# Windowed attention and a mixture of adapters: load tiles cut by key block and head instead of by running rows

## The chip, the cores and the metric

The kernel runs on one NeuronCore of one Trainium2 chip. Its engines are TensorE (PE; PEld is its weight load), VectorE (DVE), ScalarE (ACT), GpSimd (POOL) and SyncE (SP, which here only issues DMAs). The core has 16 DMA engines. The metric is the device time of one execution in microseconds; the time before is the median of three runs. A profile is of one more execution.

## The reference

q, k and v are float32 arrays of shape (8 batches, 8 heads, 576 rows, 64). The reference computes, in short:

```python
scores = q @ k.T / sqrt(64)                 # for each batch and head, 576 x 576
scores = where(abs(i - j) <= 32, scores, -1e9)
x = softmax(scores) @ v                     # (8, 8, 576, 64)
x = x.transpose(0, 2, 1, 3).reshape(4608, 512)
logits = x @ w_gate                         # 8 experts
topk, w = two best experts, softmax over their logits
out = x + sum over the two of w * ((x @ A[e]) @ B[e])   # A[e]: 512 x 16, B[e]: 16 x 512
```

Only a band of 65 keys counts for each query, so a block of 64 keys meets 128 queries at most, and a block of 128 queries meets three key blocks. The inputs are 28.3 MB, the output 9.4 MB.

## The kernel before

**Pairs.** Batch b and batch b + 4 are worked on together: one in partitions 0 to 63, the other in 64 to 127. So there are 32 units (4 pairs of batches x 8 heads) of 576 rows.

**Loads** (`load_qk` line 281, `load_v` line 321). The rows of all units are taken as one run of 18432 rows and cut into nine tiles of 2048 rows, without regard to where a head ends. A q or k tile is one DMA of 1 MB (line 288, on SP): each of 128 partitions takes 16 consecutive rows of each of the two batches, 4 KB each. Each half of it (8 rows per partition) is cast to f16 (line 299 on POOL or DVE, 297 on ACT), transposed by eight PE matmuls (line 307) into a PSUM bank, and copied into `qT` or `kT` (line 317). A v tile comes in four DMAs of 32 partitions (line 329, on POOL, which casts to f16 on the way) and is turned by one DVE transpose (line 338). The weights of the adapters come on SP once k tile 2 has been asked for (lines 253 to 258).

**Scores** (`score`, line 376). 36 tiles of eight key blocks. Two matmuls write the mask into two PSUM banks (line 393), then K^T Q is added for each block and each batch of the pair (line 398); a block whose queries lie in two q tiles takes two matmuls. ACT takes the exponential into `PT` (line 405). For the first three pairs of batches the blocks go head by head, for the last pair four heads go head by head and four block by block.

**PV** (`pv`, line 414). Up to five items (a unit and a block of 128 queries) share two PSUM banks (line 435); column 64 of v is 1 and gives the softmax sum. DVE takes the reciprocal (line 447) and writes the normalized x (line 460).

**Adapters** (`moe`, line 476). x is transposed (line 488), multiplied with all A and w_gate at once (line 529), the gate goes through nine small DVE and ACT operations (lines 539 to 560), the gated product (line 570) is transposed (579) and multiplied with all B (line 607). x is added on DVE (line 621, first pair) or by an identity matmul (line 610) with a copy on ACT or DVE (line 618). The store is on SP (line 628). Such a chain is made for ten blocks of 128 rows at once in the first three pairs of batches, and for 4, 4 and 2 blocks in the last: six chains.

**Order.** Nothing is scheduled at run time. `ORDER` lists all operations, `ON` says on which engine each runs where there is a choice, and `HOME` gives each buffer its place in its pool. Each engine works through its own operations in that order, and an instruction that waits holds up all behind it on its engine; for SP and POOL that includes the DMAs that they issue. A load also waits for a free `raw` buffer (five of 1 MB) or `v16` buffer (three). The order was written by a planner that isn't part of the kernel; durations given to `op` are its estimates and do nothing at run time.

Of the kernel before, what the change touches and what calls it, by code (L numbers as in the profile page):

```python
# [19 lines left out]
NUN = 32  # L20
NSLOT = NUN * NB
NTILE = NSLOT // 32
SB = 4
GS = 188
# [22 lines left out]
class Op:  # L47
    def __init__(self, eng, fn, bufs, need, make, prio, dma):
        self.eng, self.fn = eng, fn
        self.bufs, self.need, self.make = bufs, need, make  # L50
        self.prio, self.dma = prio, dma
        self.mode, self.count = 0, 0
        self.on, self.given = None, False


class Plan:
# [14 lines left out]
    def op(self, eng, dur, fn, bufs=(), need=(), make=(), prio=0.0, dma=0.0, mode=0, count=0):  # L71
        eng = eng if isinstance(eng, dict) else {eng: dur}
        o = Op(eng, fn, list(bufs), list(need), list(make), prio, dma)
        o.mode, o.count = mode, count
# [30 lines left out]
def kernel(  # L105
# [14 lines left out]
    POOLS = {"B": 8, "raw": 5, "c16": 6, "v16": 3,  # L120
             "qT": 3, "kT": 3, "vt": 3, "PT": 7, "xs": 2, "xT": 1, "zs": 2, "zT": 2, "ob": 4,
# [4 lines left out]
    def many(name, shape, dt, pool=sb):  # L126
# [6 lines left out]
        "qT": many("qT", [128, 2048], F16),  # L133
# [3 lines left out]
        "xs": many("xs", [128, 2, 5, DD], F16),  # L137
        "xT": many("xT", [128, 10, 4, 128], F16),
        "zs": many("zs", [128, 5, ER], F16),
        "zT": many("zT", [128, 5, 128], F16),  # L140
        "ob": many("ob", [128, 2, DD], F32),
        "sm": many("sm", [128, 280], F32),
        "rc": many("rc", [128, 5, 2, 1], F32),
# [54 lines left out]
    op("POOL", 3.5, build_mask, make=["mask"], prio=-98)  # L198
# [10 lines left out]
    op("POOL", 1.6, build_twice, make=["mask"], prio=-97)  # L209
# [35 lines left out]
    for i, t in enumerate(phys["vt"]):  # L245
# [7 lines left out]
    op("SP", 0.4, lambda: nc.sync.dma_start(  # L253
        out=waf, in_=moe_A.rearrange("e (p c) r -> p e (c r)", c=4)),
        bufs=[wb], need=[("k", 2, "raw")], make=["waf"], prio=LATE_W, dma=0.262)
    op("SP", 0.4, lambda: nc.sync.dma_start(
        out=wgf, in_=moe_w_gate.rearrange("(p c) e -> p c e", c=4)), need=[("k", 2, "raw")], make=["waf"], prio=LATE_W, dma=0.02)
    op("SP", 0.4, lambda: nc.sync.dma_start(
        out=bf, in_=moe_B.rearrange("e r d -> (e r) d")), bufs=[wb], need=[("k", 2, "raw")], make=["bf"], prio=LATE_W, dma=0.262)

# [8 lines left out]
    qrows = {"q": q, "k": k, "v": v}  # L269

    def run_view(w):

        return qrows[w].rearrange("(g b) h (n r) d -> (b h n) g (r d)", g=2, r=16)

    def v_view():

        return qrows["v"].rearrange("(g b) h (s f r) d -> (b h s) f g (r d)", g=2, f=2, r=32)

    qT, kT, vt = {}, {}, {}

    def load_qk(w, t):
        raw = buf("raw", f"raw{w}{t}")
        src = run_view(w)[128 * t:128 * t + 128]
        due = 32 * t if t else -100
        late = 0 if w == "q" else 1
        dst = buf(w + "T", f"{w}T{t}")
        (qT if w == "q" else kT)[t] = dst
        op("SP", 0.46, lambda: nc.sync.dma_start(out=ap(raw), in_=src),
           bufs=[raw], make=[(w, t, "raw")], prio=-80 + due + late if t else -200 + late, dma=DMA_MB)
        for hf in range(2):  # L290
            c16 = buf("c16", f"{w}16_{t}_{hf}")

            def cast(eng, hf=hf, c16=c16):
                o = ap(c16).rearrange("p r (g d) -> p r g d", g=2)
                i = ap(raw).rearrange("p g (f r d) -> p f r g d", f=2, d=D)[:, hf]
# [6 lines left out]
               need=[(w, t, "raw")], make=[(w, t, hf, "16")], prio=due - 30 + late + 0.1 * hf)  # L302
            tp = buf("B", f"tp{w}{t}_{hf}")

            def trans(hf=hf, c16=c16, tp=tp):
                for r in range(8):
                    nc.tensor.matmul(out=ap16(tp)[:, 128 * r:128 * r + 128], lhsT=ap(c16)[:, r],  # L307
                                     rhs=ident, is_transpose=True, start=True, stop=True)
# [4 lines left out]
            def evict(eng, hf=hf, tp=tp):  # L313

                o = ap(dst).bitcast(F32).rearrange("m (x f r) -> m f x r", f=2, r=8)[:, hf]
                i = ap(tp).rearrange("m (r x) -> m x r", r=8)
# [3 lines left out]

    def load_v(t):
        v16, dst = buf("v16", f"v16_{t}"), buf("vt", f"vt{t}")
        vt[t] = dst
        src = v_view()
        due = 32 * t if t else -90
        for g in range(2):
            for f in range(2):
                p0 = 64 * g + 32 * f
                op("POOL", 0.62, lambda p0=p0, f=f, g=g: nc.gpsimd.dma_start(  # L329
                    out=ap(v16)[p0:p0 + 32], in_=src[32 * t:32 * t + 32, f, g]),  # L330
                    bufs=[v16],
# [9 lines left out]
    for t in range(NTILE):  # L341
        load_qk("q", t)
        load_qk("k", t)
        load_v(t)


    seq = []
    for s in range(SB):
        us = list(range(8 * s, 8 * s + 8))
        if s < SB - 1:  # L350
            seq += [(u, a) for u in us for a in range(NB)]
        else:
            seq += [(u, a) for u in us[0:4] for a in range(NB)]
            seq += [(u, a) for a in range(NB) for u in us[4:8]]
    place = {ua: divmod(i, 8) for i, ua in enumerate(seq)}
    PT = {}

    def slot(u, a):
        return divmod(NB * u + a, 32)

    def run_deps(kind, u, row0, row1):

        r = set()
        for row in range(row0, row1, 32):
            t, c = divmod(NB * 64 * u + row, 2048)
            r.add((kind, t))
        return r

    def score(ti):
        ps = buf("B", f"ps{ti}", 2)  # L370
        PT[ti] = pt = buf("PT", f"PT{ti}")
        blocks = seq[8 * ti:8 * ti + 8]
        need, bufs, n = {"mask", "ident"}, {ps}, 0
        parts = []
# [369 lines left out]
```

## Time and profile before

| | before |
|---|---|
| median of 3 runs | 140.14 us (139.21 to 140.89) |
| the profiled execution | 138.75 us |
| its span | 137.0 us |
| mean granted TensorE clock | 0.969 |
| PE busy | 110.1 us (80%) |
| DVE, ACT, POOL busy | 90.3, 85.3, 49.9 us |
| moved by DMA | 33.90 MB; HBM read 28.85 MB, written 9.44 MB |
| q and k loads | 18 of 1024 KB, median 12.6 us (k) and 15.7 us (q) from issue to landing |
| v loads | 36 of 128 KB, 7.1 us to landing |

The page of the profile divides the span into 40 slices: a digit is the busy share in tenths. A line of the DMA part gives a queue with its packets, megabytes and the time that its packets took, as a share of 16 engines over the span; q1 is the queue of SP, q0 that of POOL. The megabytes of v count what is written (f16); twice as much is read. Matmuls are pipelined, so PE's busy time also holds the ends of overlapping matmuls; in the chain that ended last a matmul stands with the time from its start to the next one's.

### The profile page before, as it was taken

What the parts mean: (1) busy time and instruction counts of PE and PEld (TensorE: products, weight loads), DVE (VectorE), ACT (ScalarE), POOL (GpSimd) and SP (SyncE); (2) the same over time, 40 slices, a digit from 0 to 9 for tenths busy, and PEclk for the clock granted to TensorE, in tenths of its full rate; (3) what the DMA queues carried; (4) which work ended last, traced back from release to release, by engine and by line L of the source; (5) the groups of instructions that cost most, each with busy time, mean ns of one, the idle gap of its engine ahead of it and who ended that gap; (6) DMA issues with size and microseconds to landing.
All of it is one profiled execution on the core that took longest, in us unless ns stands there. A gap on an engine that the chain in (4) does not pass through costs nothing.

```text
span 137.0 us, 5167 instructions
## 1 busy us (share of the span) xinstructions
PE 110.1 (80%) x2238; PEld 82.2 (60%) x2238; DVE 90.3 (66%) x182; ACT 85.3 (62%) x124; POOL 49.9 (36%) x84
## 2 busy tenths in 40 slices
PE   5934777949599979299929999769999999999800
PEld 2324456637498857277717796746868676875300
DVE  2323757368586895758838987929596979768700
ACT  7104399726669697248726767748946885678620
POOL 7992187059553960559401995000000000000000
PEclk9997799999999999779999999999999999999997
DMA  4999999999999999979999499700960300636993
GB/s 100 378 292 291 360 408 334 335 384 388 255 300 386 403 299 290 286 273 251 284 326 425 89 215 232 206 13 11 334 235 5 115 5 7 234 115 240 311 369 115
DMA packets 13222, 33.90 MB, mean 247 GB/s; under 512 B 2704, under 2 KB 2704, under 8 KB 13200
## 3 DMA queue, kind: packets, MB, share of 16 engines
q1 hardware_dynamic: 11472, 28.86, 57.5%
q0 software_dynamic: 1728, 4.72, 19.4%
q8 instruction: 17, 0.28, 0.8%
q14 instruction: 5, 0.04, 0.1%
HBM read 28.85 MB, written 9.44 MB: 280 GB/s over the span
## 4 chain that ended last, share of the span: by engine, by line
PE 44%; DMA 35%; issue 6%; DVE 5%; ACT 3%; POOL 2%; SPq 1%; POOLq 0%; ACTq 0%; DVEq 0%
DMA raw<-in_k_dram 19%; DMA raw<-in_q_dram 14%; PE banks L435 9%; PE banks L398 8%; PE banks L307 6%; PE banks L488 5%; PE banks L529 5%; PE banks L607 4%; PE banks L393 4%; PE banks L610 3%; DMA out_dram<-ob 3%; POOL c L299 2%; ACT ob L618 1%; DVE xs L460 1%; PE banks L579 1%
## 5 line engine op out<-in xcount | busy, mean ns | idle before, releaser
L405 ACT ACTIVATE PT<-banks 128x1024 f16<-128x1024 f32 x36 | 36.2, 1024 | 12.4 <-PE banks L398 11.6
L299 POOL CAST c<-raw 128x1024 f16<-128x1024 f32 x27 | 27.5, 1046 | 33.1 <-DMA raw<-in_k_dram 14.6
L307 PE MATMUL banks<-ident,c 128*128 128x128 f16 x288 | 22.1, 230 | 11.1 <-POOL c L299 5.6
L307 PEld LDWEIGHTS <-c 128*128 128x128 f16 x288 | 18.3, 103 | 14.9 <-POOL c L299 6.8
L460 DVE TENSOR_TENSOR xs<-banks,rc 128x640 f16<-128x640 f32 (+1 forms) x33 | 26.4, 802 | 1.1
L398 PE MATMUL banks<-qT,kT 64*64 64x128 f16 (+3 forms) x608 | 22.8, 216 | 1.7 <-issue 1.4
L398 PEld LDWEIGHTS <-kT 64*64 64x64 f16 x608 | 17.4, 108 | 10.3 <-issue 9.9
L338 DVE STREAM_TRANSPOSE vt<-v 128x1024 f32<-128x1024 f32 x9 | 18.7, 2079 | 5.3 <-DMA v<-in_v_dram 5.3
L435 PE MATMUL banks<-vt,PT 64*128 64x65 f16 x832 | 17.5, 190 | 4.6 <-issue 3.7
L435 PEld LDWEIGHTS <-PT 64*128 64x128 f16 x832 | 14.5, 94 | 7.2 <-issue 5.3
L329 POOL DMA_DIRECT2D v<-in_v_dram x36 | 17.7, 499 | 0.1
L618 ACT COPY ob<-banks 128x1024 f32<-128x1024 f32 (+1 forms) x14 | 12.5, 928 | 5.3 <-PE banks L610 3.7
L607 PE MATMUL banks<-Bw,zT 128*128 128x512 f16 x40 | 14.9, 393 | 0.4 <-ACT zT L180 0.4
L393 PE MATMUL banks<-mask,twice 64*128 64x512 f16 x72 | 14.1, 386 | 0.6 <-ACT PT L405 0.4
L447 DVE RECIPROCAL rc<-banks 128x10 f32<-128x10 f32 (+1 forms) x33 | 7.1, 214 | 11.3 <-PE banks L435 10.1
L297 ACT CAST c<-raw 128x1024 f16<-128x1024 f32 x6 | 6.3, 1050 | 9.9 <-DMA raw<-in_q_dram 9.9
L317 ACT COPY kT<-banks 128x512 f32<-128x512 f32 x15 | 8.8, 592 | 5.2 <-PE banks L307 5.1
L610 PE MATMUL banks<-xs,ident 128*128 128x512 f16 x30 | 11.4, 379 | 0.0
L529 PE MATMUL banks<-WA,xT 128*128 128x136 f16 x160 | 10.8, 223 | 0.3 <-issue 0.3
L488 PE MATMUL banks<-ident,xs 128*128 128x128 f16 x160 | 10.8, 219 | 0.1
L488 PEld LDWEIGHTS <-xs 128*128 128x128 f16 x160 | 9.8, 114 | 1.4 <-DVE xs L460 0.2
L529 PEld LDWEIGHTS <-xT 128*128 128x128 f16 x160 | 9.8, 98 | 1.3 <-issue 0.5
(49 smaller groups left out, 97.5 us busy)
## 6 DMA issues: line engine op xcount, KB each, us to landing
raw<-in_k_dram SPq DMA_DIRECT2D x9, 1024.0 KB, 12.6
raw<-in_q_dram SPq DMA_DIRECT2D x9, 1024.0 KB, 15.7
out_dram<-ob SPq DMA_DIRECT2D x24, 256.0 KB, 3.4
v<-in_v_dram POOLq DMA_DIRECT2D x36, 128.0 KB, 7.1
out_dram<-ob SPq DMA_DIRECT2D x16, 192.0 KB, 3.0
ob<-in_moe_A_dram SPq DMA_DIRECT2D x1, 256.0 KB, 17.5
ob<-in_moe_B_dram SPq DMA_DIRECT2D x1, 256.0 KB, 10.7
wgf<-in_moe_w_gate_dram SPq DMA_DIRECT2D x1, 16.0 KB, 16.6
```

The costliest lines, as they stand in the source:

```text
L299: (nc.vector if eng == "DVE" else nc.gpsimd).tensor_copy(out=o, in_=i)
L307: nc.tensor.matmul(out=ap16(tp)[:, 128 * r:128 * r + 128], lhsT=ap(c16)[:, r], rhs=ident, is_transpose=True, start=True, stop=True)
L329: op("POOL", 0.62, lambda p0=p0, f=f, g=g: nc.gpsimd.dma_start(out=ap(v16)[p0:p0 + 32], in_=src[32 * t:32 * t + 32, f, g]), bufs=[v16], ma ...
L338: nc.vector.transpose(out=o, in_=i)
L393: nc.tensor.matmul(out=p[:, 4 * j:4 * j + 4], lhsT=twice[m], rhs=bcast(mask[m], 1, 4), start=True, stop=False)
L398: nc.tensor.matmul(out=p[m, i, c0:c0 + w], lhsT=ap(kT[t])[m, 64 * s:64 * s + 64], rhs=ap(qT[tq])[m, c:c + w], start=False, stop=(n == len( ...
L405: op("ACT", act(1024), lambda: nc.scalar.activation(out=ap(pt)[:, :, 64:192].rearrange("m i (x b r) -> m i x b r", b=2, r=16), in_=ap(ps). ...
L435: nc.tensor.matmul(out=ap(po)[:, 512 * g + VD * j:512 * g + VD * j + VD], lhsT=ap(PT[ti])[m, pos, off:off + 128], rhs=ap(vt[t])[m, sl, 0:V ...
L460: nc.vector.tensor_tensor(out=o, in0=i, in1=ap(rc)[:, 0:n].to_broadcast([128, n, 2, D]), op=ALU.mult)
L488: nc.tensor.matmul(out=ap16(tp)[:, 512 * i + 128 * c:512 * i + 128 * c + 128], lhsT=ap(xs[s])[:, b, g].rearrange("p (m c) -> p c m", c=4)[ ...
L529: nc.tensor.matmul(out=ap(pz)[:, o:o + ER + E], lhsT=ap(xT)[:, i, c, :], rhs=WA[:, c, :], start=(c == 0), stop=(c == 3))
L607: nc.tensor.matmul(out=o, lhsT=ap(zT)[:, j + i], rhs=Bw, start=True, stop=not by_pe)
```

## The change

- **q and k loads.** The tiles are cut by batch pair, row range and head. Tile t < 8 holds pair t // 2, all eight heads, and 256 rows of each: four key blocks for k; for q the range is shifted by 32 rows. Tile 8 holds what is left over of all 32 units: the ninth key block of k, and the first and last 32 rows of q. Runs are of 8 rows, 2 KB. Each half of a tile and each batch of the pair has a DMA of its own (256 KB; for q tile 8 each end too, 128 KB): 76 loads on SP instead of 18. `raw` has nine buffers of 512 KB instead of five of 1 MB.
- **v loads** are cut the same way, still four DMAs a tile on POOL.
- **Queries.** `qT` is one buffer for a pair of batches, [head, 576 rows], two in all. q tile 8 goes to a buffer `xq`, from which one copy per pair (`ends`) fills in the first and last 16 columns of pairs (32 rows) of each head.
- **Scores.** A tile is one key block of all eight heads; no block is split any more.
- **PV** takes items block by block, seven groups of 5 or 6 a pair instead of eight (nine in the last). x lies in two buffers, blocks 0 and 1 in `xa`, blocks 2 to 4 in `xb`.
- **Adapters.** Two chains for each pair, of 4 and 6 blocks of 128 rows: eight chains. The softmax pieces lie elsewhere in PSUM and SBUF.
- **Weights** are loaded from ACT's queue at the start.
- **Order.** `ORDER`, `ON` and `HOME` are new, 594 operations instead of 553. The last q or k load on SP is the first half of k tile 6, behind 12 of the 40 stores.

```diff
-    POOLS = {"B": 8, "raw": 5, "c16": 6, "v16": 3,
-             "qT": 3, "kT": 3, "vt": 3, "PT": 7, "xs": 2, "xT": 1, "zs": 2, "zT": 2, "ob": 4,
+    POOLS = {"B": 8, "raw": 9, "c16": 6, "v16": 3, "xq": 1,
+             "qT": 2, "kT": 4, "vt": 4, "PT": 7, "xa": 2, "xb": 1, "xT": 1, "zs": 2, "zT": 2, "ob": 4,
...
-        "raw": many("raw", [128, 2, 16 * D], F32),
+        "raw": many("raw", [128, 2, 8 * D], F32),
...
-    op("SP", 0.4, lambda: nc.sync.dma_start(
+    op("ACT", 0.5, lambda: nc.scalar.dma_start(
         out=waf, in_=moe_A.rearrange("e (p c) r -> p e (c r)", c=4)),
...
+    grows = {w: x.rearrange("(g b) h n d -> g b h n d", g=2) for w, x in (("q", q), ("k", k), ("v", v))}
...
+    def run_parts(w, t, f):
+
+        r = []
+        for g in range(2):
+            x = grows[w][g]
+            if t < XT:
+                r0 = 256 * (t % 2) + (32 if w == "q" else 0)
+                i = x[t // 2, :, r0:r0 + 256].rearrange("h (n f r) d -> f h n (r d)", f=2, r=8)[f]
+                r.append((g, 0, 128, i))
+            elif w == "k":
+                i = x.rearrange("b h n d -> (b h) n d")[:, 512:576].rearrange(
+                    "u (n f r) d -> f u n (r d)", f=2, r=8)[f]
+                r.append((g, 0, 128, i))
+            else:
+                for e in range(2):
+                    i = x.rearrange("b h n d -> (b h) n d")[:, 544 * e:544 * e + 32].rearrange(
+                        "u (n f r) d -> f u n (r d)", f=2, r=8)[f]
+                    r.append((g, 64 * e, 64, i))
+        return r
...
-        op("SP", 0.46, lambda: nc.sync.dma_start(out=ap(raw), in_=src),
-           bufs=[raw], make=[(w, t, "raw")], prio=-80 + due + late if t else -200 + late, dma=DMA_MB)
         for hf in range(2):
+            raw = buf("raw", f"raw{w}{t}_{hf}")
+            for n, (g, p0, np_, src) in enumerate(run_parts(w, t, hf)):
+                op("SP", 0.46, lambda g=g, p0=p0, np_=np_, src=src, raw=raw: nc.sync.dma_start(
+                    out=ap(raw)[p0:p0 + np_, g], in_=src),
+                   bufs=[raw], make=[(w, t, "raw", hf)],
...
+                if w == "q" and t < XT:
+                    c0 = 16 + 128 * (t % 2)
+                    o = ap(dst).bitcast(F32)[:, :, c0:c0 + 128].rearrange(
+                        "m h (x f r) -> m f h x r", f=2, r=8)[:, hf]
+                    i = ap(tp).rearrange("m (r h x) -> m h x r", r=8, h=NH)
...
+    def ends(s):
+
+        def go(eng):
+            w = ap(qT[s]).bitcast(F32)
+            o = dataclasses.replace(w, ap=[list(w.ap[0]), [272, 2], [288, NH], [1, 16]])
+            i = ap(xq).bitcast(F32).rearrange("m (e u r) -> m e u r", e=2, r=16)[:, :, NH * s:NH * s + NH]
+            (nc.scalar.copy if eng == "ACT" else nc.gpsimd.tensor_copy)(out=o, in_=i)
...
-                op("POOL", 0.62, lambda p0=p0, f=f, g=g: nc.gpsimd.dma_start(
-                    out=ap(v16)[p0:p0 + 32], in_=src[32 * t:32 * t + 32, f, g]),
+                x = grows["v"][g]
+                if t < XT:
+                    r0 = 256 * (t % 2)
+                    src = x[t // 2, :, r0:r0 + 256].rearrange("h (a f r) d -> f h a (r d)", f=2, r=32)[f]
+                else:
+                    src = x.rearrange("b h n d -> (b h) n d")[:, 512:576].rearrange(
+                        "u (f r) d -> f u (r d)", f=2)[f]
+                op("POOL", 0.5, lambda p0=p0, src=src: nc.gpsimd.dma_start(
+                    out=ap(v16)[p0:p0 + 32], in_=src), bufs=[v16],
...
+            for h in range(NH):
+                sl = slot(NH * s + h, a)[1]
                 for g in range(2):
                     m = slice(64 * g, 64 * g + 64)
...
+                    nc.tensor.matmul(out=p[m, h, c0:c0 + hi - lo], lhsT=ap(kT[t])[m, 64 * sl:64 * sl + 64],
+                                     rhs=ap(qT[s])[m, h, lo:hi], start=False, stop=h % 4 == 3)
...
     for s in range(SB):
+        for i0, n in ((0, 6), (6, 5), (11, 5), (16, 6), (22, 6), (28, 6), (34, 6)):
+            pv(s, i0, n)
...
     for s in range(SB):
-        e = 72 * (s + 1)
-        if s < SB - 1:
-            moe(s, [(b, g) for b in range(2) for g in range(5)], e + 16, 10)
-        else:
-            moe(s, [(b, g) for g in (0, 1) for b in range(2)], 72 * s + 66, 4)
-            moe(s, [(b, g) for g in (2, 3) for b in range(2)], 72 * s + 82, 4)
-            moe(s, [(b, g) for g in (4,) for b in range(2)], 72 * s + 90, 4)
+        moe(s, [(b, g) for g in (0, 1) for b in range(2)], 72 * s + 46, 4)
+        moe(s, [(b, g) for g in (2, 3, 4) for b in range(2)], 72 * s + 86, 4)
```

More of the change, by code (lines that the diff above doesn't have):

```diff
@@ L319, in load_qk @@
                bufs=[tp, dst], need=[(w, t, hf, "T")], make=[(w + "T", t)], prio=pr)
+    def ends(s):
[4 more added lines that the diff above has]
+            (nc.scalar.copy if eng == "ACT" else nc.gpsimd.tensor_copy)(out=o, in_=i)
+        op({"POOL": 0.45, "ACT": act(256)}, 0, go, bufs=[xq, qT[s]], need=[("qT", XT)], make=[("ends", s)],
+           prio=due_of(2 * s) + (24 if s == 0 else -10))
     def load_v(t):
@@ L428, in pv @@
                 need |= {("PT", ti), ("vt", t)}
-        last = max(x[1] for x in ops)
+        last = 9 * s + max(x[1][1] for x in ops)
         def go():
```

246 lines of the change are left out of this document (107 added, 139 removed), and 86 rows, old and new, of tables (HOME, ORDER).

## The prediction

> **What bounds the kernel now.** I read the page first, then the stretches of the span, then the chain that ended last in order of time, and last the DMA view of the first 20 us. From the page:
>
> ```profile
> span 137.0 us, 5167 instructions
> PE 110.1 (80%) x2238; PEld 82.2 (60%) x2238; DVE 90.3 (66%) x182; ACT 85.3 (62%) x124; POOL 49.9 (36%) x84
> PE   5934777949599979299929999769999999999800
> DMA  4999999999999999979999499700960300636993
> DMA packets 13222, 33.90 MB, mean 247 GB/s; under 512 B 2704, under 2 KB 2704, under 8 KB 13200
> q1 hardware_dynamic: 11472, 28.86, 57.5%
> q0 software_dynamic: 1728, 4.72, 19.4%
> PE 44%; DMA 35%; issue 6%; DVE 5%; ACT 3%; POOL 2%; SPq 1%; POOLq 0%; ACTq 0%; DVEq 0%
> DMA raw<-in_k_dram 19%; DMA raw<-in_q_dram 14%; PE banks L435 9%; PE banks L398 8%; PE banks L307 6%; PE banks L488 5%; PE banks L529 5%; PE banks L607 4%; PE banks L393 4%; PE banks L610 3%; DMA out_dram<-ob 3%; POOL c L299 2%; ACT ob L618 1%; DVE xs L460 1%; PE banks L579 1%
> ```
>
> The DMA row stands at 9 for the first half, PE's row at 7 to 9 for the second, and the chain divides likewise: a third of the span waits for q and k loads, then it is TensorE. The stretches say it with numbers (columns: stretch, length, busy us of PE, PEld, DVE, ACT, POOL, granted clock, DMA share, GB/s):
>
> ```profile
> 10.00:20.00 10.00, 6.38 (x104) 4.82 (x106) 5.45 (x7) 5.47 (x8) 3.80 (x8) 0.83 1.04 348
> 20.00:30.00 10.00, 7.49 (x188) 5.56 (x180) 6.70 (x9) 6.46 (x9) 5.00 (x7) 1.00 1.03 347
> 30.00:40.00 10.00, 8.23 (x247) 6.70 (x248) 6.47 (x13) 7.17 (x9) 7.19 (x10) 1.00 1.07 330
> 40.00:50.00 10.00, 9.35 (x171) 8.22 (x169) 8.06 (x19) 8.00 (x15) 6.63 (x11) 1.00 1.03 358
> 85.00:95.00 10.00, 8.14 (x221) 6.12 (x220) 7.31 (x15) 6.76 (x10) 0.00 (x0) 1.00 0.33 86
> 115.00:125.00 10.00, 9.92 (x138) 7.08 (x136) 7.88 (x28) 7.02 (x12) 0.00 (x0) 1.00 0.50 179
> ```
>
> Until 50 us all 16 DMA engines are full (a share of 1.03 to 1.07: the packets of an engine overlap by about 5%). After the loads the share falls to 0.3 to 0.5, and PE is full.
>
> **How a copy is dealt to the engines.** The packet counts can be taken apart. The q and k loads are 18 x 256 runs of 4 KB, the stores 4608 rows of 2 KB, the weights 1024 + 128 + 128 packets. That leaves 11472 - 10496 = 976 = 61 x 16 on q1, which has 61 issues. On q0 the 36 v loads have 32 rows each: 1728 - 1152 = 36 x 16. So every copy of this kernel closes with 16 small packets, one for each engine. The outermost counts of these copies are 128, 96 and 32, all multiples of 16, so each engine gets an equal number of rows.
>
> **The change, part by part.**
>
> *Loads.* A run is now 8 rows (2 KB), and for t < 8 the source of a q or k load is x[t // 2, :, r0:r0+256], written as h, n, (r d). The 256 rows of a head end before the next head begins, so heads and runs don't merge: the outermost count is **8 heads**, where it was 128 runs. There are 8 tiles x 2 tensors x 2 halves x 2 groups = 64 such copies of 256 KB. The v loads of t < 8 are "h a (r d)", 8 outermost too. Only tile 8 (left-over rows, 32 pairs of batch and head outermost) keeps a multiple of 16.
>
> No row shows a copy with 8 outermost. If it is dealt as the 97 copies of the trace are, in equal shares of the outermost count, there are eight shares of one head each, and eight of the 16 engines carry the load. That is my likeliest case: three different counts obey it. The bounds are 16 engines (as now) and eight.
>
> By a rule of the Trainium skill (page "DMA: Bandwidth & Descriptors", section "Why a DMA increments its semaphore by 16 and not by 1") a copy runs on the largest number up to 16 that divides the slowest dimension of both sides; on the hardware queue these are the lowest-numbered engines, on the software queue consecutive ones from a cursor that goes round. By that rule the 64 loads fall on the same eight engines each time, and the v loads alternate between the halves, which is the case that I sum below. The trace agrees for 128, 96 and 32; no run here shows 8 yet. With 16 engines instead the sum would be that of the first rival.
>
> The price. q1's packets took 0.575 x 16 x 137.0 = 1260 engine-us for 28.86 MB: 43.7 per MB, so 11.45 for a copy of 256 KB. The lower bound for 2 KB runs is the best slice of q and k loads:
>
> ```profile
> DMA  0009269999999999999999999999999999999999
> GB/s 0 0 0 106 25 197 434 434 401 393 418 303 303 303 262 361 270 311 295 311 279 271 279 270 328 295 270 279 402 287 295 418 410 401 418 410 393 434 410 418
> ```
>
> 434 GB/s over 16 engines is 36.9 us per MB. q1's mean holds as many 2 KB packets (stores) as 4 KB ones, so I take it, divided by the overlap of 1.05. What the eight busiest engines must carry before the last q or k load has landed:
> - 64 loads: 64 x 11.45 / 8 = 91.6 us (over 16 engines it would be 45.8)
> - tile 8 of q and k, 2.10 MB over 16: 5.7; weights, 0.54 MB: 1.5
> - v: 0.194 x 16 x 137.0 = 425 engine-us, on an average engine 26.6
> - stores: in the new order 12 of 40 (2.88 MB) stand ahead of the last load (k tile 6, first half) on SP: 7.9
>
> Sum 133.3, over 1.05 = 127.0. The first load gives the start:
>
> ```profile
> 0.74 4.98 DMA raw<-in_k_dram
> ```
>
> 1 MB over 16 engines takes 2.9 of these 4.98 us, so data flows from 0.74 + 2.1 = 2.8 us. The last load lands at about **130 us**; in the kernel before DMA was no longer full by 85 us.
>
> Do queues leave these engines idle? SP issues 116 copies instead of 61 at some 0.4 us, 50 us in 130. A load waits on SP for a raw buffer, and there are nine of 512 KB, up to 18 copies or 26 us of work ahead. The stores on SP wait for adapter chains and hold back the loads behind them; but those chains need tiles that were issued more than ten copies earlier, so the reserve covers them. I take no idle time; without that cover it is a few us.
>
> *What is left after the last load.* k tile 6 holds the first four key blocks of the last batch pair. Its second group of transposes stands on PE ahead of all nine score tiles of that pair. Before, the like point is the last k transposes:
>
> ```profile
> 105.05 0.45 PE banks L307 x8
> 108.45 0.51 PE banks L435 x26
> 108.96 0.21 PE banks L393 x2
> 109.17 0.56 PE banks L398 x16
> 121.62 0.22 PE banks L607
> 121.83 0.22 PE banks L610
> 122.05 0.95 PE banks L529 x16
> 123.00 0.22 PE banks L579 x4
> 123.22 0.45 PE banks L488 x8
> 124.57 1.02 ACT ob L618
> 127.25 3.44 DMA out_dram<-ob
> 130.79 1.01 ACT ob L618
> ```
>
> From 105.5 to the end are 31.5 us. By these rows PE still had 6 score tiles (0.78: 4.7 us), 208 PV matmuls (4.1), 40 transposes (2.25), 40 low-rank matmuls (2.4), 20 of zs (1.1) and 10 pairs of output matmuls at 0.87 (8.7): 23.2 us. The other 8.3 are waits: for a softmax, for norm on DVE, the last gate chain, and the output copy with its store. After the change there stand behind that point 9 score tiles (7.1), 264 PV matmuls (5.2), 64 transposes (3.6), 64 low-rank matmuls (3.8), 16 of zs (0.9), 8 transposes of q (0.45) and the output matmuls of both chains of the last two pairs, 40 (8.7): 29.7 us. With the same 8.3 of waits 38.0. Before it come the cast and the transposes:
>
> ```profile
> L299 POOL CAST c<-raw 128x1024 f16<-128x1024 f32 x27 | 27.5, 1046 | 33.1 <-DMA raw<-in_k_dram 14.6 <-DMA raw<-in_q_dram 13.1 <-PE banks L307 4.7
> L237 ACT COPY PT<-zt__115 128x256 f32<-128x256 f32 x8 | 2.7, 398 | 0.0
> L557 DVE RECIPROCAL sm<-sm 128x10 f32<-128x10 f32 x3 | 0.6, 216 | 0.1
> L553 DVE SCALAR_TENSOR_TENSOR sm<-sm,banks 128x80 f32<-128x80 f32 x3 | 0.7, 230 | 0.4 <-ACT banks L547 0.4
> ```
>
> 1.05 + 0.45 + 0.1 between them = 1.6.
>
> *The other parts* are small and lie under the load waits. Score tiles of whole blocks: 608 matmuls become 576, 1.1 us less PE at 0.56 / 16. Reciprocal and norm run 28 times instead of 33, on the same elements: about 1 us less DVE. Eight chains instead of six: 80 small DVE operations instead of 69, 11 x 0.22 = 2.4 us more DVE. The four copies of left-over queries are like the copy of 256 elements in the row above: 4 x 0.4, on POOL and ACT. The weights now come first, on ACT's queue: their 1.5 us are in the sum. The q eviction writes another pattern with the same 512 elements; neither gain nor loss is excluded, 18 x 0.1 us either way is my bound. If PE bound throughout they would be worth about 2 us; with PE waiting for data, nothing.
>
> **Sum.** 129.8 + 1.6 + 38.0 = 169.4 us of span. The profiled execution took 138.75 for its span of 137.0, 1.75 around it, and lies 1% under the median of 140.14. So 171.2; **forecast 171 us**, 1.22 times the median before. With 36.9 us per MB in place of 43.7 / 1.05 the loads end at 115 and it is 157; without overlap they end at 136 and it is 178, and some 5 us of idle queues make 183.
>
> **Rivals.**
> 1. *All 16 engines carry the new loads*, whether a copy is cut below the head or eight shares wander over the engines. For it: the DMA rows show nothing but even use. Against it: every copy that they show has an outermost count that 16 divides. Then the engine time is (733 + 91 + 24 + 425 + 126) / 16 / 1.05 = 83.3 us, the last load lands at 86, and 86.1 + 1.6 + 38.0 + 1.75 = **127 us**, up to 135 if PE, with some 66 us of work before that point, isn't ready by then. This is the side on which it is faster; it decides whenever the 64 loads use more than about 12 engines, where their term falls from 91.6 to 61 and the time to about 142.
> 2. *The v loads fall on one half.* They are eight heads outermost as well. If they all sit on the engines of the q and k loads, 32 / 36 of 26.6 = 23.6 us come twice: + 22.5, **194 us**. If they all sit on the other eight, 22.5 less: 149. Nothing in the rows speaks for either.
> 3. *The change isn't what ends last*: that the reordered tail with its last chain of six items costs more than the 8.3 us of waits. It is 3 us at most (a third gate chain of about 2 us is gone, an add per pair remains), inside the range of every case.
>
> **How the numbers follow.** Forecast's case, 157 to 183: 0.70. Rival 1: 0.13. Rival 2: 0.12, half on each side. The remaining 0.05 is for stalls on SP or POOL beyond the reserve, above 183. The range 150 to 195 holds the forecast's case and most of rival 2, a little over 8 in 10, and leaves rival 1 out. Faster by over 1% (about what a measurement of this kernel tells from no change) has rival 1 almost alone: 0.11; within 1%: 0.02; slower: 0.87.
>
> **What would show it.** Right: a DMA row near 5 or 6 instead of 9 for most of the span at some 200 to 270 GB/s, loads until about 130 us, q and k landings well over 15 us, more waiting of POOL, ACT and DVE for raw, and q1 with fewer than 16 small packets for each of the 64 loads. Wrong: a DMA row at 9 with 330 GB/s until about 85 us; then rival 1 holds. If the loads end at 130 but the time isn't near 171, it is the 38 us behind them that I have mis-sized.

## The result, and the profile after

The changed kernel takes 179.19 us (median of 4, 176.21 to 180.37) where the kernel before, on the same chip, takes 139.97 (139.21 to 140.89). The ratio is 1.265, with a 95% interval of 1.248 to 1.283; it goes by the executions in the faster of the two states of this chip (176.21 and 178.09 us of the four), so it is less than 179.19 / 139.97. The forecast was 171 us, range 150 to 195. The profiled execution took 178.09 us for a span of 176.3.

From the first page of the changed kernel, in the order in which the prediction read the page of before (the three rows of digits are busy tenths and GB/s in 40 slices):

```profile
span 176.3 us, 5204 instructions
PE 123.9 (70%) x2206; PEld 89.6 (51%) x2206; DVE 89.9 (51%) x186; ACT 86.3 (49%) x123; POOL 50.9 (29%) x85
PE   4800487629619879469998997807947999986660
DMA  3876656779659569865556669778939030373086
GB/s 108 192 185 221 180 184 221 216 211 232 152 187 241 159 204 227 190 242 211 204 208 256 229 191 244 264 277 272 231 101 321 0 122 14 124 231 106 26 308 204
q1 hardware_dynamic: 15168, 28.32, 45.7%
q0 software_dynamic: 2752, 4.72, 15.8%
DMA 58%; PE 24%; DVE 7%; SPq 3%; ACT 3%; issue 1%; POOLq 1%; DVEq 0%; ACTq 0%
```

The DMA row was a line of nines until half time; now it stands mostly between 5 and 8, with a 9 here and there, for three quarters of a longer span, at some 200 GB/s. Bytes and compute are nearly the same. PE has gone from 110.1 to 123.9 us of busy time with 32 matmuls fewer, at a mean granted clock of 0.868 instead of 0.969: busy time times clock is 107.5 and 106.7. The clock was lower in stretches in which PE had gaps, as in the first of these two (stretch, length, busy us of PE, PEld, DVE, ACT, POOL, granted clock, DMA share, GB/s):

```profile
20.00:30.00 10.00, 6.85 (x80) 4.67 (x79) 5.44 (x7) 5.48 (x8) 2.54 (x3) 0.64 0.60 199
140.00:150.00 10.00, 10.00 (x204) 7.07 (x202) 7.69 (x18) 7.86 (x11) 0.00 (x0) 1.00 0.18 64
```

Between 20 and 30 us the kernel before had a DMA share of 1.03 and 347 GB/s; here it is 0.60 and 199. From the chain that ended last (start, us, what), its first steps and those around the last load:

```profile
1.60 7.88 DMA raw<-in_k_dram
9.49 11.46 DMA raw<-in_q_dram
...
110.05 10.29 DMA raw<-in_q_dram
120.35 12.52 DMA raw<-in_k_dram
133.01 1.06 POOLq L756
```

The chain is load upon load, but for 75.2 to 99.4 us, where it runs over PE, ACT and DVE, until the last one lands at 120.35 + 12.52 = 132.9 us; the forecast said 130. A copy of 256 KB takes 8 to 13 us in the steps shown.

**How many engines.** By the way in which the prediction took the counts apart, q1 has 9216 packets of 2 KB for q and k and 4608 for the stores. 15168 - 13824 = 1344 small packets are left. The 12 copies of tile 8 and the 40 stores account for 52 x 16 = 832, and 1344 - 832 = 512 = 64 x 8. Each of the 64 copies with 8 heads outermost closes with eight small packets. Here the trace agrees with what the prediction cited from the Trainium skill (page "DMA: Bandwidth & Descriptors", section "Why a DMA increments its semaphore by 16 and not by 1"): eight outermost, eight engines. The time of the packets says the same. Queue q1 from 2.8 to 132.9 us in the changed kernel:

```profile
q1 hardware_dynamic: 11751, 22.18, 48.4%
```

0.484 x 16 = 7.7 engines at a time, with twelve stores and the copies of tile 8 among them. Where the chain leaves the loads, the same share is 57.8% (75 to 99 us), so the eight weren't idle there. Which eight they are can't be seen in the records.

On q0 the count goes another way: 2752 - 1152 = 1600 = 32 x 48 + 4 x 16, which fits 48 small packets instead of 16 for each v copy with eight outermost.

### The profile page after: what moved, and what is told of

The parts are those of the page before. It is cut to its first block, busy times and chain, and to the rows that moved or that the text cites. A ratio compares the mean times of both kernels' runs of the same rounds, so it can differ in the third digit from the quotient of the medians.

```text
span 176.3 us, 5204 instructions
## 1 busy us (share of the span) xinstructions
PE 123.9 (70%) x2206; PEld 89.6 (51%) x2206; DVE 89.9 (51%) x186; ACT 86.3 (49%) x123; POOL 50.9 (29%) x85
## 3 DMA queue, kind: packets, MB, share of 16 engines
q1 hardware_dynamic: 15168, 28.32, 45.7%
q0 software_dynamic: 2752, 4.72, 15.8%
## 4 chain that ended last, share of the span: by engine, by line
DMA 58%; PE 24%; DVE 7%; SPq 3%; ACT 3%; issue 1%; POOLq 1%; DVEq 0%; ACTq 0%
DMA raw<-in_q_dram 35%; DMA raw<-in_k_dram 23%; PE banks L422 5%; PE banks L468 4%; SPq L308 3%; PE banks L513 3%; PE banks L627 3%; PE banks L329 3%; PE banks L416 3%; DVE xb L487 2%; PE banks L630 2%; PE banks L553 1%; DVE ob L641 1%; PE banks L603 1%; DVE zs L594 1%
## 5 line engine op out<-in xcount | busy, mean ns | idle before, releaser
L329 PE MATMUL banks<-ident,c 128*128 128x128 f16 x288 | 26.2, 251 | 26.5 <-ACT c L319 15.1
L329 PEld LDWEIGHTS <-c 128*128 128x128 f16 x288 | 21.0, 113 | 30.2 <-ACT c L319 16.6
L422 PE MATMUL banks<-qT,kT 64*64 64x128 f16 (+1 forms) x576 | 24.5, 230 | 1.2 <-ACT qT L355 1.0
L638 ACT COPY ob<-banks 128x1024 f32<-128x1024 f32 x13 | 13.0, 1013 | 18.5 <-issue 7.4
L487 DVE TENSOR_TENSOR xb<-banks,rc 128x768 f16<-128x768 f32 x16 | 15.1, 956 | 2.0 <-PE banks L513 1.5
L480 DVE RECIPROCAL rc<-banks 128x12 f32<-128x12 f32 (+1 forms) x28 | 6.2, 220 | 15.5 <-PE banks L468 15.3
L487 DVE TENSOR_TENSOR xa<-banks,rc 128x640 f16<-128x640 f32 (+1 forms) x12 | 10.4, 869 | 5.8 <-PE banks L513 5.3
L345 ACT COPY qT<-banks 128x512 f32<-128x512 f32 x13 | 7.6, 590 | 11.8 <-PE banks L329 11.8
L181 ACT COPY xT<-banks 128x512 f32<-128x512 f32 x16 | 9.2, 588 | 6.7 <-PE banks L513 6.6
L321 DVE CAST c<-raw 128x1024 f16<-128x1024 f32 x3 | 2.1, 694 | 18.6 <-DMA raw<-in_q_dram 18.6
```

The source lines that it names most:

```text
L321: (nc.vector if eng == "DVE" else nc.gpsimd).tensor_copy(out=o, in_=i)
L422: nc.tensor.matmul(out=p[m, h, c0:c0 + hi - lo], lhsT=ap(kT[t])[m, 64 * sl:64 * sl + 64], rhs=ap(qT[s])[m, h, lo:hi], start=False, stop=h ...
L487: nc.vector.tensor_tensor(out=o, in0=i, in1=ap(rc)[:, 0:n].to_broadcast([128, n, 2, D]), op=ALU.mult)
L638: (nc.vector.tensor_copy if eng == "DVE" else nc.scalar.copy)(out=ap(ob)[:, 0:m], in_=i0)
```

## The experiments

Three questions were put: is it the number of engines; if so, what makes up the rest; and does the order of the work matter. All runs compare with the kernel before on the same chip.

**1. Give the loads sixteen engines.** The q and k source of tiles 0 to 7 becomes 2048 consecutive rows, so that 128 runs are outermost:

```diff
+                if w in "qk":
+                    r0 = 2048 * (t % 2)
+                    i = x[t // 2].rearrange("h n d -> (h n) d")[r0:r0 + 2048].rearrange(
+                        "(p f r) d -> f p (r d)", f=2, r=8)[f]
```

> The changed kernel, but the q and k loads of t < 8 take 2048 consecutive rows of a batch (128 equal runs, outermost count 128) instead of 256 rows of each of eight heads; same copies, packets, bytes and order. Rows stand under wrong heads, so the attention isn't the reference's; the work is the same. Eight engines (my theory): the sum of rival 1 holds, 127 to 135 us, the last q or k load lands near 86 us, each such copy closes with 16 small packets. 2 KB packets or 76 copies are what is slow: 175 to 180 us, nothing moves. The new order is what is slow: 175 to 180 us as well.

Measured: 146.22 us (144.9 to 146.56), ratio 1.043 [1.033, 1.053]. Rows of its page:

```profile
span 144.8 us, 5204 instructions
DMA  2999999999999999899857899995830432650485
q1 hardware_dynamic: 15680, 28.32, 60.4%
```

The nines are back, q1 has 15680 - 13824 = 1856 = 116 x 16 small packets, and 33 of the 39 us are gone. Yet it is not the 127 to 135 us of the first rival: experiments 4 to 6 look at that.

**2. The same for k alone** (`if w in "k"` in the same lines).

> The same for the k loads alone (32 of the 64 copies). Eight engines: 32 x 11.45 x (1/8 - 1/16) / 1.05 = 21.8 us less than the changed kernel, some 157 us. A threshold (the slowest copies set the pace whatever the rest does): 170 or more. 2 KB packets, copies or order: 175 to 180 us.

Measured: 167.11 us (166.46 to 168.17), ratio 1.197 [1.184, 1.210]. Only 12 of the 33 us come back when half of the loads is cured.

```profile
q1 hardware_dynamic: 15424, 28.32, 54.8%
```

One reason stands in this row: 0.548 x 16 x 164.7 = 1444 engine-us for 28.32 MB is 51.0 per MB, where the changed kernel has 0.457 x 16 x 176.3 = 1289, 45.5 per MB. With 51.0 the prediction's own sum for the low eight engines is (68.7 + 5.7 + 7.9) x 51.0 / 43.7 + 28.1 = 124.1, over 1.05 and with the start 121 us (68.7 is 45.8 for q on eight plus 22.9 for k on sixteen; 28.1 are the weights and v). The last cast of a q or k tile starts at 121.4 us in this run (its row stands further down). Why the packets are longer here than in the changed kernel was not tried; in experiment 1, with sixteen engines for q and k, a megabyte costs 49.4, so that the mixture is the reason isn't shown.

**3. The reverse, on the kernel before**: the same tiles and order, only the q and k sources dealt in 8, 16 or 32 groups. Each 1 MB load becomes two copies, whose rows are taken in groups that overlap (other rows than the reference's, some twice), so that the outermost dimensions don't merge:

```diff
-        op("SP", 0.46, lambda: nc.sync.dma_start(out=ap(raw), in_=src),
+        def load():
+            for g in range(2):
+                i = src[:, g]
+                run = i.ap[0][0]
+                i = dataclasses.replace(i, ap=[[15 * run, 8], [run, 16], list(i.ap[-1])])
+                nc.sync.dma_start(out=ap(raw)[:, g], in_=i)
+        op("SP", 0.46, load,
```

> The kernel before, with each q or k load read as 8 groups of 16 runs that lie 15 runs apart, one copy for each batch of the pair (36 copies of 512 KB, 4 KB packets, old order). Some rows are read twice and others not at all, so the output isn't the reference's; bytes and packets are as before. Eight engines: q and k take 18.9 x 43.7 / 8 = 103 us of the eight, with weights, v and 4 stores 134 / 1.05 = 127, the last load lands at 130, and 1.6 + 38 + 1.75 behind it give 171 us. Packet size or order as the cause: 140 us, as both are those of before.

> Control: the same with 16 groups of 8 runs that lie 7 runs apart. Eight engines as the cause: 139 to 142 us, like before. Rows that are read twice, runs that don't merge, or 36 copies as the cause: as slow as the kernel with 8 groups, about 171 us.

> The kernel before, each q or k load as 32 groups of 4 runs that lie 3 runs apart (36 copies of 512 KB, some rows read twice, others not at all, so the output isn't the reference's). The run with 16 groups of 8 was not the clean control that I took it for: its 4 KB packets took 268 ns instead of 173, with all 16 engines in use. Theory A, where the rows land: consecutive shares of 8 partitions for each engine collide, and 32 groups of 4 are dealt as 128 rows are: 139 to 143 us, packets of 170 to 180 ns. Theory B, runs that don't merge, rows read twice or 36 copies: 160 to 166 us as with 16 groups.

Measured: 8 groups 182.25 us (179.52 to 186.51), ratio 1.287 [1.269, 1.305]; 16 groups 164.56 us, 1.178 [1.166, 1.189]; 32 groups 141.69 us, 1.022 [1.013, 1.030]. The pages, first of 8 groups, then of 16, then of 32:

```profile
span 177.7 us, 5202 instructions
DMA  2985555765666576586755597559776732024696
q1 hardware_dynamic: 11472, 28.86, 45.2%
```

```profile
span 162.3 us, 5202 instructions
DMA  4999999999999999999999999699317530073794
q1 hardware_dynamic: 11760, 28.86, 66.1%
```

```profile
span 141.1 us, 5202 instructions
DMA  3999999999999999978999269910662300545893
q1 hardware_dynamic: 11760, 28.86, 56.0%
```

Eight outermost makes the kernel before as slow as the changed one, with all else in place. The small packets are 11472 - 10496 = 976 = 36 x 8 + 43 x 16 with 8 groups and 11760 - 10496 = 1264 = 79 x 16 with 16 and 32. Queue q1 with 8 groups, from 20 to 60 us:

```profile
q1 hardware_dynamic: 2352, 7.18, 48.7%
```

That is 0.487 x 16 = 7.8 engines. The 16 groups were meant as the control and weren't one. All sixteen engines are full (nines until 60% of the span), but a megabyte costs 0.661 x 16 x 162.3 / 28.86 = 59.5 engine-us, against 0.560 x 16 x 141.1 / 28.86 = 43.8 with 32 groups and 0.452 x 16 x 177.7 / 28.86 = 44.5 with 8. The 32 groups overlap in their source rows too, and cost nothing of the kind; so the next run asks for the same in the changed kernel.

**4. Sixteen groups in the changed kernel.** Only the two outer dimensions of the source are exchanged; the rows of a tile stand in another order, and so other queries and keys meet:

```diff
-                i = x[t // 2, :, r0:r0 + 256].rearrange("h (n f r) d -> f h n (r d)", f=2, r=8)[f]
+                i = x[t // 2, :, r0:r0 + 256].rearrange("h (n f r) d -> f n h (r d)", f=2, r=8)[f]
```

> The kernel after with only the two outer dimensions of the q and k source of tiles 0 to 7 exchanged: 16 groups of rows outermost, each with 8 heads inside, where it was 8 heads with 16 groups inside. The bytes read, the 2 KB runs and the tiles are the same; the rows land in another order in the tile, so queries and keys are permuted and the sums mix other rows. Theory A, from b_16 (16 groups of eight neighbouring partitions: 16 engines full, but 164.6 us where 32 groups took 141.7): all sixteen engines carry the loads (small packets on q1 rise from 1344 to 1856), yet the packets lengthen and the time falls only to 158 to 170 us, the 146.2 us of a_qk16 plus about the 23 us between b_16 and b_32. Theory B: the number of engines is all that counts, b_16 was slow by its overlapping source rows, and the time is that of a_qk16, 145 to 149 us.

Measured: 152.33 us (151.91 to 153.17), ratio 1.105 [1.093, 1.118].

```profile
span 150.7 us, 5204 instructions
DMA  5999999999999999999998899997460302670485
q1 hardware_dynamic: 15680, 28.32, 64.5%
```

It lies between the two theories, and neither range holds it. Here no source row is read twice, and still the price is 0.645 x 16 x 150.7 / 28.32 = 54.9 per MB where experiment 1 has 0.604 x 16 x 144.8 / 28.32 = 49.4. So sixteen full engines are not yet sixteen quick ones, and a higher price doesn't need overlapping source rows. But the rise is 5.5 here and was 15.7 between 32 and 16 groups, with packets of another size, so it isn't excluded that the overlap added to it there. The price per megabyte is shown; its cause isn't. The records of a packet have neither its engine nor its addresses, so which partitions, or which places of the memory behind, the engines of such a copy meet at one time can't be read from them.

**5. What is left of the loss: the size of the runs, and v.** The kernel before with each load as two copies of 2 KB runs, 128 outermost:

```diff
+            for f in range(2):
+                nc.sync.dma_start(out=ap(raw)[:, :, 512 * f:512 * f + 512], in_=src[:, :, 512 * f:512 * f + 512])
```

> The kernel before, each q or k load as two copies of 512 KB with 2 KB runs (first 8 rows of every run, then the last 8), outermost count 128; same data, same order. With the q and k loads of the changed kernel spread over 16 engines, q1 took 60.4% of the span for 28.32 MB, 49.4 engine-us per MB, against 43.7 before. If the 2 KB runs are the cause: 18.9 MB x 5.7 / 16 = 6.7 us later loads, 143 to 147 us. If it is copies dealt in different ways side by side: 139 to 142 us.

Measured: 141.72 us (140.31 to 142.96), ratio 1.013 [1.002, 1.024]. That is about one third of what experiment 1 has left. Whether it is the 2 KB runs isn't shown: this kernel also issues two copies for each load where there was one, and the two copies of 4 KB runs of experiment 3 with 32 groups cost 2.2%.

The v loads were tried both ways: dealt in 8 groups in the kernel before (each copy of 32 rows as 8 groups of 4, 3 rows apart), and from consecutive rows in the kernel of experiment 1.

> The kernel before, each v load as 8 groups of 4 runs that lie 3 runs apart: outermost count 8 on POOL's queue (some rows read twice, others not at all, so the output isn't the reference's). This is rival 2 by itself. If the eight engines alternate from copy to copy, as the skill's page has it for the software queue: 139 to 144 us. If they are always the same eight: v takes 425 / 8 = 53 us of them instead of 26.6, the loads end 25 us later, 160 to 166 us.

> The changed kernel with the q, k and v loads of t < 8 all from 2048 consecutive rows of a batch, so that no load of it has an outermost count of 8; rows stand under wrong heads, the output isn't the reference's, the work is the same. If the 6 us that remain over the kernel before (146.2 against 140.4) come from the v loads: 138 to 142 us. If from 2 KB runs, or from loads that stand behind stores on SP: 145 to 147 us.

Measured: b_v8 139.44 us (136.16 to 141.82) beside 138.8 for the kernel before in the same comparison, no difference that can be told; a_qkv16 147.81 us, ratio 1.064 [1.055, 1.073], not less than the 1.043 of experiment 1. The row of q0 of b_v8 (in a_qkv16 it has 1728 packets, 16 small ones for each copy, as before):

```profile
q0 software_dynamic: 2880, 4.73, 18.8%
```

2880 - 1152 = 36 x 48: the 48 small packets of an eightfold v copy show here as well, and cost no time. The second rival of the prediction (v on one half of the engines, 194 or 149 us) has nothing to stand on.

**6. The order of the work.** In experiment 1 the last q or k load was issued at 91.3 us, behind stores that waited on SP. Here the last ten load pieces are moved ahead of eight stores in the order by hand, in the kernel of experiment 1 and in the changed kernel as it is:

```diff
-ORDER = (... 215, ... 208, 244, ... 248, ... 243, ... 238, ... 209, ... 239, ... 234, ... 218, ... 219, ...
+ORDER = (... 215, 208, 244, 248, 243, 238, 209, 239, 234, 218, 219, ...
```

> The kernel after with the q and k loads of tiles 0 to 7 taken from 2048 consecutive rows (the edit of a_qk16, whose rows come under the wrong heads), and in the order by hand the last ten of these load pieces moved ahead of the eight stores that stood between them on SP; casts, matmuls and everything else stay in their order. In a_qk16 the last q/k load was issued at 91.3 us and SP had waited 33.5 us for output tiles before stores. Theory 1: what is left of the loss once all sixteen engines carry the loads (146.2 against 140.4 us) comes from loads held behind stores in SP's queue: the last load is issued before 82 us and the time is 136 to 141 us. Rival: the loads were early enough, and the rest lies at the start (first score after the weights), in the 2 KB runs and in the tail: the last load comes earlier but the time stays at 144 to 148 us.

> The kernel after, complete, with the same ten load pieces moved ahead of the eight stores on SP. If the eight engines that carry the q and k loads bound the time, the order on SP buys little: the last q/k load still lands at 128 to 133 us and the time is 174 to 180 us. If SP's order is what delays the loads, it falls by about the 10 us that stores held SP in the stretch from 92 to 120 us, to 166 to 171 us.

Measured: 151.17 us (148.5 to 152.26) beside 140.09 for the kernel before, so 3 to 5 us slower than experiment 1 (by ratio or by median); and for the changed kernel 183.34 us (181.59 to 186.39), ratio 1.310 [1.296, 1.324], 4 us slower than it was. No theory said slower. The loads did come earlier: the last cast of a q or k tile starts at 94.2 us instead of 100.9, and at 125.8 instead of 133.0. The waits of the changed kernel with the new order (who waited for what: us, times, longest), and one of its stretches:

```profile
ACT ob L638 <- DMA out_dram<-ob: 17.9, 1, 17.9
PE banks L416 <- ACT ob L638: 17.4, 1, 17.4
```

```profile
110.00:120.00 10.00, 0.00 (x0) 0.00 (x0) 0.00 (x0) 0.00 (x0) 4.03 (x6) 0.50 0.73 279
```

In the changed kernel the gain of 7 us at the loads is paid back with interest: stores that now stand behind the loads land late, an output copy on ACT waits 17.9 us for its output tile, the PSUM banks that it would free keep the next score tile waiting, and PE does nothing for a whole stretch. A store was not only an obstacle for the loads behind it; it frees what PE needs. In the kernel of experiment 1 with this order the like waits are shorter (ACT 3.9 us for an output tile, PE 3.4 us behind it), and whether they are all of its loss isn't shown.

**7. The weights.** They come first in the changed kernel. In the kernel of experiment 1 their three loads are moved to about 22 us:

```diff
-ORDER = (26, 23, 3, 24, ... 35, 25, ... 268, ...
+ORDER = (23, 3, ... 268, 26, 24, 25, ...
```

> The kernel a_qk16 (after, q and k loads of tiles 0 to 7 from consecutive rows, under the wrong heads) with its three weight loads issued from ACT's queue at about 22 us instead of first, as the kernel before issued them from SP at 21.8 us. In a_qk16 TensorE was busy 18.2 us of the first 30, in the kernel before with its copies halved to 2 KB runs (b_2kb) 21.6 us. Theory: the weights ahead of the first loads cost the start those 3.4 us: PE is busy over 20.5 us of the first 30 and the time is 141.5 to 144 us, a ratio of 1.01 to 1.03 to the kernel before. Rival: the late start is made up by the time that TensorE is full from 60 us on, and the rest lies behind it, in the coupling of stores and output tiles and in the tail: 145 to 147.5 us, 1.035 to 1.05.

Measured: 150.84 us (149.64 to 151.99), ratio 1.082 [1.073, 1.090]: slower again. The stretches show which half of the theory held:

```profile
0.00:10.00 10.00, 6.51 (x8) 2.52 (x8) 2.70 (x11) 1.99 (x3) 6.96 (x25) 1.00 0.79 218
10.00:20.00 10.00, 5.92 (x76) 4.41 (x76) 4.76 (x6) 5.99 (x9) 0.70 (x1) 0.83 1.07 255
20.00:30.00 10.00, 8.01 (x188) 6.07 (x190) 5.33 (x12) 5.39 (x9) 8.90 (x14) 1.00 1.08 339
30.00:40.00 10.00, 5.32 (x133) 4.06 (x131) 3.59 (x5) 4.32 (x6) 4.31 (x7) 0.76 0.77 184
```

PE does 20.4 us in the first 30, about the 20.5 that the theory asked for. From 30 to 40 it does 5.3, and DMA drops to 0.77: the weights' casts stand in ACT's order at a place that the late weights no longer meet (ACT is idle for 3.8 us before the first of them, waiting for A), and what waits behind them on ACT is held up. By 40 us the start is given back: PE has done 25.8 us, in experiment 1 25.7. Why the end comes 4.6 us later than there isn't shown.

## Why the prediction came out as it did

**Eight outermost, eight engines: shown.** By the packet count (64 x 8), by experiment 1 (cured), and by experiment 3 (the same loss in the kernel before by this alone). The prediction reasoned from three counts that all were multiples of 16, and from a rule that it could not yet see. Experiment 3 with 32 groups, which has the same two dimensions and the same two copies, excludes that the form of the source alone is the cause.

**The loads' sum: right within 3 us.** 129.8 against 132.9. The mis-sized term is the price: 45.5 engine-us per MB instead of 43.7. With it the sum is (91.6 + 5.7 + 7.9) x 45.5 / 43.7 + 28.1 = 137.6, over 1.05 and with 2.8 of start 133.9. The best price of before (36.9 per MB, the 157 us end of the range) was not the mean of any kernel here; that end also scaled the v loads and the weights by it, and with the terms of q1 alone it is 160.

**SP: right in the main that it hides, low in its size.** The chain has SPq at 3% of the span, mostly one issue of 4.6 us at 68.9 us, while q1 keeps its eight engines busy. I took 0.4 us for issuing a load. The instructions that touch raw in the changed kernel (duration min/median/max in ns, first and last start in us):

```profile
L308 SPq DMA_DIRECT2D raw<-in_q_dram x40: 529/599/3557, 0.7 to 116.5; - x40
```

and in experiment 1, where sixteen engines are used:

```profile
L312 SPq DMA_DIRECT2D raw<-in_q_dram x40: 327/427/1477, 0.7 to 85.8; - x40
```

0.60 us against 0.43 at the median, but that isn't the number of engines in the main. With 16 groups in the changed kernel (experiment 4), sixteen engines are used too, and the source has two outer dimensions that don't merge, as in the changed kernel:

```profile
L308 SPq DMA_DIRECT2D raw<-in_q_dram x40: 536/544/1379, 0.7 to 91.2; - x40
```

So some 0.12 us go with the two dimensions, and 0.06 are left for eight engines or for a queue that is fuller.

**Behind the last load: 39.6 forecast, 43.4 measured.** This is the step that carries most of the error in proportion. My counts stood: the groups of PE after 133 us hold 144 score matmuls, 264 of PV, 64 transposes, 64 low-rank matmuls, 16 of zs and 40 output matmuls. The stretches from that point to the end, first of the kernel before, then the two of the changed kernel in which PE isn't full:

```profile
105.50:137.00 31.50, 24.20 (x462) 16.44 (x462) 20.11 (x62) 19.01 (x28) 0.00 (x0) 0.97 0.47 164
```

```profile
157.00:161.00 4.00, 2.28 (x34) 1.81 (x31) 2.34 (x5) 1.10 (x3) 0.00 (x0) 1.00 0.76 248
161.00:168.00 7.00, 4.90 (x45) 2.95 (x46) 4.91 (x19) 3.13 (x7) 0.00 (x0) 1.00 0.12 44
```

Before, PE was busy for 24.2 and idle for 7.3. After, by the same view in five stretches, it is busy for 32.5 and idle for 10.8. So PE's work grew by 8.3 where I had 29.7 + 0.45 - 23.2 = 7.0. Of the 10.8 idle, 1.1 lie in the cast; the other 9.7 took the place of 7.3 (the 8.3 of waits in the forecast, less the 1.0 by which its count of PE work fell short of 24.2). The 1.3 us of work and the 2.4 of waits are the error of this step, and carrying the waits over is the larger part. Behind PE's last matmul there are as many us as before: 6.2 (130.8 to 137.0) and 6.0 (170.3 to 176.3). The added waits lie in the two stretches shown, in which PE is idle for 1.7 + 2.1 = 3.8 us. There the last chain has small DVE and ACT steps to run, and the chain of work shows it (start, us):

```profile
157.82 0.96 DVE xb L487
159.02 0.97 DVE xb L487
...
162.53 0.70 DVE zs L594
...
165.32 0.97 DVE zs L594
```

During the two norms, and the two gates one after the other, PE has too little to put beside them. The third rival named this tail and bounded it at 3 us; it is 3.7 to 3.8. The sum of the errors, 3.1 + 3.8, is the whole difference between 171.2 and the profiled 178.1.

**The tail also explains why the first rival's 127 us was not to be had.** POOL makes the last casts of q and k. Its casts in the changed kernel, in the kernel with k cured, and with q and k cured (duration min/median/max in ns, first and last start in us):

```profile
L321 POOL CAST c<-raw x26: 1037/1043/1112, 26.7 to 133.0; 128x1024 f16<-128x1024 f32 x26
```

```profile
L325 POOL CAST c<-raw x26: 1034/1041/1127, 26.1 to 121.4; 128x1024 f16<-128x1024 f32 x26
```

```profile
L325 POOL CAST c<-raw x26: 1040/1042/1134, 23.0 to 100.9; 128x1024 f16<-128x1024 f32 x26
```

From the last of them to the end of the span there are 176.3 - 133.0 = 43.3 us, 164.7 - 121.4 = 43.3, and 144.8 - 100.9 = 43.9; with 16 groups 150.7 - 106.3 = 44.4. In these four kernels the same tail follows. In experiment 1 it begins at 100.9 and not at the rival's 86. Its price of 49.4 per MB alone would put the rival's sum at 93.4, an estimate ((733 + 91 + 126) x 49.4 / 43.7 + 449 = 1523, over 16 and 1.05, and 2.8); loads that wait behind stores fit the rest. When they don't (experiment 6), the last cast is at 94.2, and the tail is 54 us long (148.6 - 94.2), as PE isn't ready.

The stretches of experiment 1 say where PE falls behind; the last row is the kernel before:

```profile
0.00:50.00 50.00, 32.25 (x508) 22.77 (x508) 22.37 (x44) 23.59 (x36) 27.64 (x55) 0.87 1.00 280
50.00:101.00 51.00, 49.59 (x1033) 37.25 (x1030) 39.47 (x84) 37.45 (x53) 22.17 (x31) 0.96 0.91 264
```

```profile
0.00:50.00 50.00, 38.19 (x718) 28.43 (x719) 29.52 (x56) 30.31 (x45) 31.42 (x60) 0.97 1.00 328
```

From 50 us to the last cast PE is busy for 49.6 of 51 us, so in that time earlier loads would gain next to nothing. At 50 us it has done 32.3 of its 115.8 us; without a single gap after that it ends at 133.5 us, which is 135 us of time. The prediction's condition, "if PE isn't ready by then", was the case, and its 135 us as an end were still too low.

**The small edits: about 4%, mostly at the start.** Of the ratio of 1.265, 1.265 - 1.105 = 0.160 goes when sixteen engines carry the loads in 16 groups, a further 0.062 when 128 rows are outermost, and 0.043 stays. Of that, b_2kb had about 0.013. The two stretches above point to the start for most of it: by 50 us experiment 1 has made 508 matmuls where the kernel before has made 718, and afterwards its PE is idle for 11.3 us in all, against 15.1. The loads come in more slowly there. Queue q1 from 3 to 20 us, in experiment 1 and in the kernel before:

```profile
q1 hardware_dynamic: 1860, 3.28, 77.8%
```

```profile
q1 hardware_dynamic: 1212, 4.70, 69.4%
```

That is 0.778 x 16 x 17 / 3.28 = 64.5 engine-us per MB against 40.2. Without the weights in front (experiment 7) it is still 0.869 x 16 x 17 / 3.86 = 61.2; what makes these packets long, the left-over tiles that are read there among others, was not tried. Costing these edits at nothing did no harm that shows while DMA bounds, as in the changed kernel as it is, and would not have been right with the loads cured.

No version tried beats the kernel before. A layout that keeps this change's tiles and has 32 or more rows outermost would need another order of rows within a tile, with its transposes and masks; it was not built.

## What to carry to other kernels

Write down the outermost count of each copy's source as it stands after dimensions have merged, before and after a change: a slice that keeps a head's rows from running on into the next can turn 128 into 8 with the same bytes, and that alone added a quarter or more to the time here (1.287 in the kernel before). Then look at the count of small packets on the queue and at the engine time per megabyte: a full DMA row says that the engines are occupied, not that they are quick (59.5 against 43.8 engine-us per MB in two kernels with full rows). Time loads and stores as one system: what is moved forward on a queue moves something else back, and a late store can stop an engine by way of the tile it would have freed.

## What the runs showed of the hardware that I had not expected

- Sixteen engines on sixteen groups of eight rows: 59.5 engine-us per MB (16 groups) against 43.8 (32 groups) with 4 KB runs, and 54.9 against 49.4 with 2 KB runs.
- Issuing a copy from SP took 0.43 us at the median where most sources have one outer dimension of 128 (experiment 1), 0.54 with two outer dimensions on sixteen engines (experiment 4), and 0.60 with two on eight.
- The counts fit 48 small packets instead of 16 for an eightfold copy on the software queue, at no cost in time that could be told (139.44 against 138.8 us).
- The price of a megabyte on q1 with loads of 2 KB runs was not one number: 45.2 in b_2kb (0.586 x 16 x 139.2 / 28.86), 45.5 in the changed kernel, 49.4 in experiment 1 and 51.0 in experiment 2. No run tells why.
